# The output product of a Fourier-mixing and gated-FFN kernel: 15 products over three row blocks in place of 7 over two

## The chip, the cores and the metric

The kernel runs on one core of a Trainium2 chip. The metric is the device time of one execution in microseconds (us), the median of three runs: 2009.69 us for the kernel before (2009.16 to 2014.03). All arithmetic is fp32.

## What is computed

The input `x` is (8, 3008, 256): 8 batches of 3008 rows. A two-dimensional Fourier transform over rows and features is taken and its real part kept; the 24064 rows that result go through a gated feed-forward layer with 1536 hidden features.

```
X = np.fft.fft(x, axis=1)
X = np.fft.fft(X, axis=2)
x = X.real.astype(np.float32).reshape(B * S, D)
gate = 1.0 / (1.0 + np.exp(-(x @ w_gate)))
val = x @ w_val
return (gate * val @ w_out).astype(np.float32)
```

## The kernel before

**Symmetry.** Row k and row 3008-k of the transform share their work. For each batch the kernel makes three arrays over k = 0..1504 (1505 columns, features on the partitions): P (`pk`), Q (`qk`) and E (`ek`), where E is the one feature that folding 256 features to 128 leaves over; it is the same in all partitions. The transform over features is merged into the gate and value weights once, at the start (`merge`, L247), giving `G1`, `G2` and the per-feature factors `ge`, which a small DMA takes from row 0 of `G2` (L257). With A = G1'P + ge E and B = G2'Q, the pre-activations of row k are A+B and those of row 3008-k are A-B.

**Chunks and iterations.** The 1505 columns of a batch are cut into chunks of CH = 256 (five of 256, one of 225). For each chunk the main loop (from L691) runs over 12 tiles of 128 hidden features: one iteration `i` per batch, chunk and tile, 576 in all. TensorE and the other engines get their instructions in the order in which this loop writes them, so each engine's queue is in that order. An iteration does:

- `seed` (L447): ScalarE (VectorE in the first chunk) writes ge E into a PSUM bank `pf`, two iterations ahead; gate and value share the bank. `psx` has four such banks.
- `front_a` (L458): TensorE adds G1'P, so that the bank holds A.
- `twice` (L463): ScalarE copies 2A to SBUF (`ae`).
- `front_b` (L469): TensorE adds G2'Q: the bank holds A+B.
- `gate_a` (L474), for the tile before: ScalarE's sigmoid of the gate half, VectorE's 2A-(A+B) = A-B (`z`, L484) and the product gate x value (`h`, L485). `gate_b` (L487): the second sigmoid (L492) and product (`h`, L493), for the mirrored row.

**The output product.** Two feature tiles make a pair. For a pair the output product has 2 row blocks (k and 3008-k) x 2 feature tiles x 2 output halves = 8 matrix products of 128x128 by 128xCH; the kernel takes 7 by the Strassen-Winograd scheme. Four sums per pair of the `h` blocks are made on GpSimd (`sf`, L495 to L499), the weight sums once in `forms` (L260) on GpSimd. `back` (L508) issues the 7 matmuls in two parts, 3 and 4, over the two iterations 2p+4 and 2p+5, into four PSUM banks `po` that accumulate over the chunk's six pairs.

**The end of a chunk.** `finish` (L528): ScalarE copies the products from PSUM to `c` (L522, L580); then a list `later` is worked off one entry per iteration: five sums on GpSimd (L582 to L586), four 32x32-block transposes on VectorE (`flip`, L540) and stores. For the last chunk of all the sums are made on VectorE, from PSUM (L566 to L575).

**Beside it.** The next batch's input is folded on GpSimd, one operation per iteration (`fold_ops`, L282 to L311), and once per batch TensorE makes the next P and Q in one burst (`whole`, L383), in the `po` banks. In the first 50 us, and during the first chunk, the weights are unpacked, merged and turned into their sums. In the start, `half` (L344) also runs matmuls of `dt` against itself into the unused columns of the banks `ev` and `od`.

An fp32 matmul shows in the profile as two instructions, each with its own weight load; below each of them is called a pass. Almost all matmuls bear L102, the line of the helper `mm`.

Of the kernel before, what the change touches and what calls it, by code (L numbers as in the profile page):

```python
# [45 lines left out]

NQ = 6
NP = 126
HP = 64
HUGE = float((2 ** 24 - 1 - 2 ** 20) * 2.0 ** -7)  # L50
# [3 lines left out]
def kernel(  # L54
# [21 lines left out]
    CH = 256  # L76
# [5 lines left out]
    assert F % WC == 0 and D == WC and NFT % 2 == 0 and stab.shape == (NP, 2, NQ, NE + NO)  # L82
# [9 lines left out]
    app = ctx.enter_context(tc.tile_pool(name="app", bufs=3))  # L92
    zp = ctx.enter_context(tc.tile_pool(name="zp", bufs=3))
    hp = ctx.enter_context(tc.tile_pool(name="hp", bufs=3))
    sp = ctx.enter_context(tc.tile_pool(name="sp", bufs=2))
    cp = ctx.enter_context(tc.tile_pool(name="cp", bufs=2))
    op = ctx.enter_context(tc.tile_pool(name="op", bufs=2))
    psx = ctx.enter_context(tc.tile_pool(name="psx", bufs=4, space=PSUM))
# [50 lines left out]
    wf = const.tile([P, NPR, 7, P], F32, name="wf")  # L149
# [7 lines left out]
    ed = dram.tile([B - 1, NK], F32, name="ed")  # L157
# [23 lines left out]
    def weight_load(j):  # L181
# [7 lines left out]
        def some(n, pool, tag):  # L189

            key = tag, (j - 6) // 3 if tag == "c7" else 0
            if key not in shared:
                shared[key] = pool.tile([P, n, 2 * WC], F32, name=f"w{tag}", tag=tag)
            return shared[key]

        if j < KEEP:
            pool, tag = ((zp, "z"), (pqp, ("pk", "qk", "ek")[j % 3]), (op, "os"), (sp, "sf"))[
                j // 3 if j < 6 else j // 2 - 1]
            raw = pool.tile([P, 2, WC, 2], I32, name="raw", tag=tag)
            if j < 6:  # L200
                pool, tag = ((app, "ae"), (hp, "h"))[j // 3]
                ws = pool.tile([P, 2, WC], F32, name="ws", tag=tag)
            else:
                ws = some(3, cp, "c7")[:, (j - 6) % 3].rearrange("p (c f) -> p c f", c=2)
        else:
            both = some(12, xp, "x4")
            r, i = (j - KEEP) % 3 * 2, 6 + (j - KEEP) % 6
            raw = both[:, r : r + 2].rearrange("p a n -> p (a n)").bitcast(I32).rearrange(
                "p (c f w) -> p c f w", c=2, w=2)
            ws = both[:, i].rearrange("p (c f) -> p c f", c=2)  # L210
# [28 lines left out]

    def weight_use(j, other=None):  # L240
        w, c = jobs[j]
        if w == 2:
            forms(WS.pop(j), c)
        else:
            merge(WS.pop(j), w, c, other)
# [14 lines left out]
    def forms(ws, c):  # L260

        w = ws.rearrange("p f (a h j) -> p f h a j", h=2, j=TB)
        f = wf[:, c].rearrange("p m (a j) -> p m a j", j=TB)
        sub = lambda o, a, b: nc.gpsimd.tensor_tensor(o, a, b, op=ALU.subtract)
        nc.scalar.copy(f[:, 0:2], w[:, :, 0])
        nc.scalar.copy(f[:, 2], w[:, 1, 1])
        sub(f[:, 4], w[:, 0, 1], w[:, 0, 0])
        sub(f[:, 6], w[:, 1, 1], w[:, 0, 1])
        sub(f[:, 5], w[:, 1, 1], f[:, 4])
        sub(f[:, 3], w[:, 1, 0], f[:, 5])  # L270
# [73 lines left out]
    def half(w, d, blk, sn, other=None):  # L344
# [3 lines left out]
        full = [bank(name, other and other[i]) for i, name in enumerate(("ev", "od"))]  # L348
        ev, od = [sum_[:, 0:n] for sum_ in full]

        def sums(*qs):
            for q in sorted(qs, key=lambda q: q % 2):
                mm((ev, od)[q % 2], w(q), ST[0][0:NP, int(sn), q, c0 : c0 + n], q < 2, q >= NQ - 2)
            if other is None and NQ - 1 in qs:

                for sum_ in full:
                    mm(sum_[:, n:], dt[:, 0, 0:P], dt.rearrange("p c d -> p (c d)")[:, n:], False, True)
# [25 lines left out]
    def whole(b, blk, what):  # L383
        _, then, both = seq_group(b, blk, what, (2, 1) if what else (3, 0))
        both()
        return then()

    def seq_start(b):
        PQE[b] = (pqp.tile([P, NK], F32, name="pk", tag="pk"),
                  pqp.tile([P, NK], F32, name="qk", tag="qk"),  # L390
                  pqp.tile([P, NK], F32, name="ek", tag="ek"))
        if b:
            nc.sync.dma_start(out=PQE[b][2], in_=ed[b - 1 : b, :].to_broadcast([P, NK]))
# [15 lines left out]
    def e_sums():  # L409


        ps = bank("pe", 3)
# [8 lines left out]
        er = cp.tile([P, NK], F32, name="er", tag="c7")[0:m]  # L421
# [5 lines left out]
        def rest():  # L427
# [3 lines left out]
            nc.scalar.dma_start(out=ed, in_=er)  # L431
# [3 lines left out]
    chunks = [(k0, min(CH, NK - k0)) for k0 in range(0, NK, CH)]  # L435
    pairs = [(b, c, i) for b in range(B) for c in range(len(chunks)) for i in range(NPR)]
    H, SF = {}, {}

    def cut(i):
        b, c, _ = pairs[i // 2]  # L440
        k0, n = chunks[c]
        f = i % (2 * NPR)
        return PQE[b], slice(k0, k0 + n), n, f, slice(f * P, (f + 1) * P)

    PF, AP, Z = {}, {}, {}

    def seed(i):  # L447

        (_, _, ek), ks, n, f, _ = cut(i)
        PF[i] = bank("pf").rearrange("p (g n) -> p g n", g=2)[:, :, 0:n]  # L450
        for g in range(2):
            if i < 2 * NPR:
                nc.vector.tensor_scalar(out=PF[i][:, g], in0=ek[:, ks],  # L453
                                        scalar1=ge[:, g, f : f + 1], scalar2=None, op0=ALU.mult)
            else:
                nc.scalar.activation(PF[i][:, g], ek[:, ks], AF.Copy, scale=ge[:, g, f : f + 1])  # L456

    def front_a(i):  # L458
        (pk, _, _), ks, _, _, fs = cut(i)
        for g in range(2):  # L460
            mm(PF[i][:, g], G1[:, g, fs], pk[:, ks], False, True)

    def twice(i):  # L463

        n = cut(i)[2]
        AP[i] = app.tile([P, 2, CH], F32, name="ae", tag="ae")[:, :, 0:n]
        nc.scalar.activation(AP[i], PF[i], AF.Copy, scale=2.0)  # L467

    def front_b(i):  # L469
        (_, qk, _), ks, _, _, fs = cut(i)  # L470
# [3 lines left out]
    def gate_a(i):  # L474

        n = cut(i)[2]
        p, fh = i // 2, i % 2
        z = Z[i] = zp.tile([P, 3, CH], F32, name="z", tag="z")[:, :, 0:n]
        if fh == 0:
            H[p] = hp.tile([P, 2, 2, CH], F32, name="h", tag="h")[:, :, :, 0:n]  # L480
            SF[p] = sp.tile([P, 4, CH], F32, name="sf", tag="sf")[:, :, 0:n]
        pf = PF.pop(i)
        nc.scalar.activation(z[:, 2], pf[:, 0], AF.Sigmoid)  # L483
        nc.vector.tensor_tensor(z[:, 0:2, ::-1], AP.pop(i), pf, op=ALU.subtract)  # L484
        nc.vector.tensor_tensor(H[p][:, fh, 0], z[:, 2], pf[:, 1], op=ALU.mult)  # L485

    def gate_b(i):  # L487

        p, fh = i // 2, i % 2
        z, h, s = Z.pop(i), H[p], SF[p]  # L490
        tt = nc.gpsimd.tensor_tensor
        nc.scalar.activation(z[:, 0], z[:, 0], AF.Sigmoid)  # L492
        nc.vector.tensor_tensor(h[:, fh, 1], z[:, 0], z[:, 1], op=ALU.mult)  # L493
        if fh == 0:
            tt(s[:, 2], h[:, 0, 0], h[:, 0, 1], op=ALU.subtract)  # L495
        else:
            tt(s[:, 0], h[:, 0, 1], h[:, 1, 1], op=ALU.add)  # L497
            tt(s[:, 1], s[:, 0], h[:, 0, 0], op=ALU.subtract)  # L498
            tt(s[:, 3], h[:, 1, 0], s[:, 1], op=ALU.subtract)  # L499


    SLOT = {1: (3, 0), 2: (0, 0), 6: (0, 1), 5: (1, 0), 7: (1, 1), 4: (2, 1), 3: (2, 0)}
    ORDER = ((1, 2, 4), (6, 3, 7, 5))
    FIRST = {1, 2, 4, 7}
    PO = []
    later = []

    def back(p, part):  # L508
        b, c, i = pairs[p]
        n = chunks[c][1]  # L510
        if part == 0 and i == 0:
# [257 lines left out]
```

## Time and profile before

| what | value |
|---|---|
| time, median of 3 | 2009.69 us |
| profiled span | 2006.7 us |
| first iteration of the main loop starts at | 51.0 us |
| second chunk (iteration 12) starts at | 114.5 us |
| one full chunk afterwards, 180 passes of 256 columns | 38.8 us |
| a batch's last chunk, 180 passes of 225 columns, the first of them still of 256 | 34.9 us |
| a burst for the next P and Q | 11.9 us |
| last matmul ends, last store lands | 1999.3 us, 2006.7 us |

The page lists, for each engine, its busy time and, for each group of instructions, how many there were, the busy time, the mean duration of one, and for how long the engine had stood idle before them. A matmul's duration in it includes the pipeline behind the array; what a stream of matmuls costs is read from the distance between their starts. VectorE is DVE there, ScalarE ACT, GpSimd POOL; PEld are TensorE's weight loads.

### The profile page before, as it was taken

Reading aid. Unit: us, or ns where it says so; the run is one execution under the profiler, and the core shown is the slowest. Engines: PE = TensorE matmul, PEld = TensorE weight load, DVE = VectorE, ACT = ScalarE, POOL = GpSimd, SP = SyncE. Lnnn points to the kernel's source line nnn. Section 1 sums busy time; section 2 is a strip of 40 time slices with the busy share of each in tenths; the row PEclk is TensorE's granted clock in tenths of the full one; section 3 lists DMA queues with packets and bytes.
Section 4 is the critical chain, followed back from the end, with each engine's and each line's share of the span. In section 5 each row is a group of like instructions: output and inputs, shape, how many; then the busy total and the mean of one; then the engine's idle time right before and its main releaser. Section 6 shows DMA issues by size and latency. Waiting matters only on the chain.

```text
span 2006.7 us, 27514 instructions
## 1 busy us (share of the span) xinstructions
PE 1971.3 (98%) x9520; PEld 1740.7 (87%) x9520; DVE 1093.4 (54%) x2093; ACT 1332.4 (66%) x3156; POOL 1285.5 (64%) x1704
## 2 busy tenths in 40 slices
PE   6899999999999999999999999999999999999998
PEld 4688789888998889888898888988899888998888
DVE  7655546554555456554565545555455544554555
ACT  3566657675777567775677656766577665777765
POOL 3577757774786457864677646876477754655554
PEclk9999999999999999999999999999999999999999
DMA  7253412112011020202011021111200000000001
GB/s 266 81 128 82 151 32 102 49 29 74 11 47 47 27 74 17 72 18 90 11 42 52 13 88 22 43 41 37 74 11 11 20 27 12 11 20 12 11 17 26
DMA packets 160811, 100.29 MB, mean 50 GB/s; under 512 B 128419, under 2 KB 151715, under 8 KB 157994
## 3 DMA queue, kind: packets, MB, share of 16 engines
q1 hardware_dynamic: 158850, 98.00, 16.8%
q8 instruction: 75, 1.23, 0.2%
q10 hardware_dynamic: 1822, 0.54, 0.1%
q14 instruction: 64, 0.52, 0.1%
HBM read 73.74 MB, written 50.17 MB: 62 GB/s over the span
## 4 chain that ended last, share of the span: by engine, by line
PE 96%; DMA 2%; DVE 1%; ACT 1%; issue 0%; ACTq 0%; DVEq 0%
PE pf L102 48%; PE po L102 42%; PE ev L102 4%; DMA ge<-G 1%; PE ps L102 1%; DMA st<-in_stab_dram 1%; PE od L102 0%; DVE pf L453 0%; DMA raw<-in_moe_w_gate_dram 0%; DVE z L484 0%; ACT ae L467 0%; PE pe L102 0%; ACT z L492 0%; ACT G L254 0%; ACT z L483 0%
## 5 line engine op out<-in xcount | busy, mean ns | idle before, releaser
L484 DVE TENSOR_TENSOR z<-ae,pf 128x512 f32<-128x512 f32 (+1 forms) x576 | 389.6, 676 | 615.3 <-ACT z L483 615.2
L102 PE MATMUL pf<-pk,G 128*128 128x256 f32 (+1 forms) x2304 | 582.7, 375 | 6.0 <-DVE pf L453 6.0
L102 PE MATMUL pf<-qk,G 128*128 128x256 f32 (+1 forms) x2304 | 582.9, 375 | 5.2 <-ACT ae L467 5.2
L456 ACT ACTIVATE pf<-ek,ge 128x256 f32<-128x256 f32 (+1 forms) x1128 | 532.1, 472 | 18.3
L102 PE MATMUL po<-sf,wf 128*128 128x256 f32 (+1 forms) x2304 | 534.6, 375 | 0.0
L497 POOL TENSOR_TENSOR sf<-h 128x256 f32<-128x256 f32 (+1 forms) x288 | 206.8, 718 | 474.5 <-DVE h L493 474.5
L467 ACT ACTIVATE ae<-pf 128x512 f32<-128x512 f32 (+1 forms) x576 | 339.2, 589 | 248.2 <-PE pf L102 248.1
L102 PEld LDWEIGHTS pf<-pk,G 128*128 128x128 f32 x2304 | 436.7, 190 | 59.3 <-DVE pf L453 7.0
L102 PEld LDWEIGHTS pf<-qk,G 128*128 128x128 f32 x2304 | 438.0, 190 | 57.0 <-ACT ae L467 7.2
L102 PEld LDWEIGHTS po<-sf,wf 128*128 128x128 f32 x2304 | 437.7, 190 | 49.8 <-POOL sf L499 0.4
L493 DVE TENSOR_TENSOR h<-z 128x256 f32<-128x256 f32 (+1 forms) x576 | 348.1, 604 | 190.4 <-ACT z L492 188.6
L102 PE MATMUL po<-h,wf 128*128 128x256 f32 (+1 forms) x1728 | 413.7, 375 | 1.6 <-ACT a L429 1.6
L483 ACT ACTIVATE z<-pf 128x256 f32<-128x256 f32 (+1 forms) x576 | 218.2, 379 | 259.8 <-PE pf L102 253.3
L102 PEld LDWEIGHTS po<-h,wf 128*128 128x128 f32 x1728 | 328.8, 190 | 39.2 <-ACT a L429 2.0
L495 POOL TENSOR_TENSOR sf<-h 128x256 f32<-128x256 f32 (+1 forms) x288 | 206.4, 717 | 139.6 <-PE po L102 58.8
L492 ACT ACTIVATE z<-z 128x256 f32<-128x256 f32 (+1 forms) x576 | 233.1, 405 | 17.4 <-DVE z L484 17.3
L485 DVE TENSOR_TENSOR h<-z,pf 128x256 f32<-128x256 f32 (+1 forms) x576 | 235.1, 408 | 0.0
L498 POOL TENSOR_TENSOR sf<-sf,h 128x256 f32<-128x256 f32 (+1 forms) x288 | 208.2, 723 | 22.6
L499 POOL TENSOR_TENSOR sf<-h,sf 128x256 f32<-128x256 f32 (+1 forms) x288 | 207.5, 721 | 22.6
L102 PE MATMUL ev<-st,x 63*128 63x376 f32 (+4 forms) x372 | 97.7, 414 | 6.0 <-DVE x L292 5.8
L102 PE MATMUL od<-st,x 63*128 63x376 f32 (+4 forms) x372 | 96.8, 412 | 0.0
L102 PEld LDWEIGHTS ev<-st,x 63*128 63x128 f32 (+1 forms) x372 | 66.2, 187 | 32.8 <-DVE x L292 6.2
(98 smaller groups left out, 938.7 us busy)
## 6 DMA issues: line engine op xcount, KB each, us to landing
x<-xr SPq DMA_DIRECT2D x14, 1536.0 KB
out_dram<-os SPq DMA_DIRECT2D x288, 64.0 KB
xr<-in_xf_dram SPq DMA_DIRECT2D x14, 768.0 KB
xr<-in_xf_dram SPq DMA_DIRECT2D x35, 256.0 KB
ek<-ed SPq DMA_DIRECT2D x7, 752.5 KB
out_dram<-os SPq DMA_DIRECT2D x92, 56.0 KB
x<-in_xf_dram SPq DMA_DIRECT2D x2, 1512.0 KB
tr<-in_stab_dram SPq DMA_DIRECT2D x2, 1129.5 KB
```

The lines of the kernel that those rows point to most:

```text
L102: nc.tensor.matmul(o, l, r, start=start, stop=stop, skip_group_check=True)
L456: nc.scalar.activation(PF[i][:, g], ek[:, ks], AF.Copy, scale=ge[:, g, f : f + 1])
L467: nc.scalar.activation(AP[i], PF[i], AF.Copy, scale=2.0)
L483: nc.scalar.activation(z[:, 2], pf[:, 0], AF.Sigmoid)
L484: nc.vector.tensor_tensor(z[:, 0:2, ::-1], AP.pop(i), pf, op=ALU.subtract)
L485: nc.vector.tensor_tensor(H[p][:, fh, 0], z[:, 2], pf[:, 1], op=ALU.mult)
L492: nc.scalar.activation(z[:, 0], z[:, 0], AF.Sigmoid)
L493: nc.vector.tensor_tensor(h[:, fh, 1], z[:, 0], z[:, 1], op=ALU.mult)
L495: tt(s[:, 2], h[:, 0, 0], h[:, 0, 1], op=ALU.subtract)
L497: tt(s[:, 0], h[:, 0, 1], h[:, 1, 1], op=ALU.add)
L498: tt(s[:, 1], s[:, 0], h[:, 0, 0], op=ALU.subtract)
L499: tt(s[:, 3], h[:, 1, 0], s[:, 1], op=ALU.subtract)
```

## The change

Three feature tiles now make a group, and the 2n rows of a chunk are cut into three row blocks of R = 2n/3 rows. A group's output product is 3 row blocks x 3 feature tiles x 2 output halves = 18 matrix products of 128x128 by 128xR, for which a scheme with 15 products is used. It is meant to lower the number of columns that TensorE streams for an output row. So that rows divide by three, chunks have 252 columns (the last of a batch 246).

What goes with it:

- 13 sums of `h` blocks per group on GpSimd (`H_SUMS`), of R elements; 11 sums and 4 copies of weights per group (`W_SUMS`, `W_COPIES`), once.
- `back` in three parts of five products, over iterations 3p+5 to 3p+7. The products fill five PSUM banks, so three are left for `pf`.
- At the end of a chunk 20 sums of R elements (`C_SUMS`) on VectorE in place of five on GpSimd; `later` is worked off three entries per iteration. ScalarE copies five banks instead of four.
- E: from the second chunk on each chunk gets its own rows of E by a DMA (`e_rows`), eight iterations ahead. In the first chunk there is no seed: E stands in row 0 of Q, so that `front_b` adds it, and VectorE makes A in SBUF (`part`).
- The filling matmuls of `dt` are gone, `app` and `zp` have two buffers in place of three, `cp` and `op` one in place of two, and the staging of the weights (`home`) uses other buffers. The folding is spread evenly over 60 iterations (42 for the first two).

```diff
+H_SUMS = {1: ((9, 3, 0, 0), (10, 3, 6, 0), (11, 7, 1, 0), (12, 7, 4, 0), (13, 4, 9, 0), (14, 6, 11, 0),
+              (15, 4, 6, 1)),
+          2: ((11, 8, 11, 0), (12, 8, 12, 0), (9, 5, 9, 0), (10, 10, 5, 0), (16, 2, 11, 0),
+              (16, 9, 16, 0))}
...
+PRODUCTS = ((0, 12), (1, 11), (4, 9), (6, 4), (2, 13), (5, 5), (13, 0), (8, 6), (11, 2), (12, 8), (9, 3),
+            (10, 10), (14, 1), (15, 7), (16, 14))
+PLACE = (0, 1, 2, 5, 3, 4, 6, 7, 8, 9, 10, 11, 14, 13, 12)
+C_SUMS = (((8, 1, 8, 0), (1, 1, 0, 0), (3, 3, 1, 0), (0, 0, 10, 1), (4, 4, 0, 1), (1, 6, 2, 0),
+           (4, 4, 1, 0), (10, 14, 8, 1), (7, 7, 10, 0), (11, 0, 11, 0), (11, 11, 5, 0), (5, 5, 7, 1)),
+          ((9, 9, 8, 0), (9, 13, 9, 1), (9, 9, 2, 0), (12, 9, 12, 0), (12, 11, 12, 1), (14, 9, 14, 0),
+           (11, 11, 6, 0), (13, 13, 11, 1)))
...
-    CH = 256
+    NG = NFT // 3
+    CH = 252
+    NB = 1 + max(b // 3 for b in PLACE)
...
-    psx = ctx.enter_context(tc.tile_pool(name="psx", bufs=4, space=PSUM))
+    psx = ctx.enter_context(tc.tile_pool(name="psx", bufs=8 - NB, space=PSUM))
...
+        for i, (a, b, op) in enumerate(W_SUMS):
+            nc.gpsimd.tensor_tensor(f[:, i], block(a), block(b), op=(ALU.subtract, ALU.add)[op])
+        for i, (a, sign) in enumerate(W_COPIES):
+            nc.scalar.mul(f[:, len(W_SUMS) + i], block(a), float(sign))
...
-            if other is None and NQ - 1 in qs:
-
-                for sum_ in full:
-                    mm(sum_[:, n:], dt[:, 0, 0:P], dt.rearrange("p c d -> p (c d)")[:, n:], False, True)
...
+        EK[i // NFT] = ekp.tile([P, CH], F32, name="ek", tag="ek")[:, 0:n]
+        nc.sync.dma_start(out=EK[i // NFT], in_=ed[b : b + 1, k0 : k0 + n].to_broadcast([P, n]))
...
+        for g in range(2 if i >= NFT else 0):
+            nc.scalar.activation(PF[i][:, g], EK[i // NFT], AF.Copy, scale=ge[:, g, f : f + 1])
...
+        if i >= NFT:
+            nc.scalar.activation(AP[i], PF[i], AF.Copy, scale=2.0)
+            return
         for g in range(2):
+            nc.vector.scalar_tensor_tensor(out=AP[i][:, g], in0=pqe[2][:, ks],
+                                           scalar=ge[:, g, f : f + 1], in1=PF[i][:, g],
+                                           op0=ALU.mult, op1=ALU.add)
...
+        for dst, a, b, op in H_SUMS.get(fh, ()):
+            nc.gpsimd.tensor_tensor(block(p, dst), block(p, a), block(p, b),
+                                    op=(ALU.subtract, ALU.add)[op])
...
+        for at_, (hb, wb) in list(enumerate(PRODUCTS))[part * 5 : part * 5 + 5]:
+            t, j = divmod(PLACE[at_], 3)
+            mm(PO[t][:, j * R : (j + 1) * R], wf[:, g, wb], block(p, hb), g == 0 and at_ % 3 == 0,
+               g == NG - 1)
+            if g == NG - 1 and at_ % 3 == 2:
...
+                nc.scalar.copy(C[0][:, 3 * t * R : 3 * (t + 1) * R], PO[t][:, 0 : 3 * R])
...
+            nc.vector.tensor_tensor(*v, op=(ALU.subtract, ALU.add)[op])
...
+        for h in range(2):
+            later.extend([lambda x=x: sum_(*x) for x in C_SUMS[h]])
+            later.append(lambda h=h: flip(0, h))
+            later.append(lambda h=h: (flip(1, h), h and (store(0), store(1))))
...
+    nc.scalar.dma_start(out=ed[0:1], in_=PQE[0][2][0:1])
+    nc.scalar.copy(PQE[0][1][0:1, 0:CH], PQE[0][2][0:1, 0:CH])
...
+        f0, steps = (s0 - 2 * i0, 5 * i0) if b > 1 else (s0 - 4, 42) if b else (i0 + 8, 42)
...
-        if i >= 4:
-            back(i // 2 - 2, i % 2)
+        if i >= 5:
+            back((i - 5) // 3, (i - 5) % 3)
...
-        if later:
-            later.pop(0)()
+        for f in later[0:3]:
+            f()
+        del later[0:3]
...
-    for p in range(len(pairs) - 2, len(pairs)):
-        for part in range(2):
-            back(p, part)
+    for i in range(count, count + 5):
+        back((i - 5) // 3, (i - 5) % 3)
```

## What the change will do, predicted

> **What bounds the kernel now.** I read the page's busy shares and its chain of waits first:
>
> ```profile
> PE 1971.3 (98%) x9520; PEld 1740.7 (87%) x9520; DVE 1093.4 (54%) x2093; ACT 1332.4 (66%) x3156; POOL 1285.5 (64%) x1704
> ...
> PE 96%; DMA 2%; DVE 1%; ACT 1%; issue 0%; ACTq 0%; DVEq 0%
> ```
>
> TensorE is busy for 98% and is 96% of the chain. A busy share could hide stretching, so next the list of waits, for TensorE alone from 130 to 2000 us:
>
> ```profile
> PE po L102 <- ACT a L429: 1.6, 1, 1.6
> PE pf L102 <- ACT ae L467: 1.0, 1, 1.0
> ```
>
> That is all: 2.6 us in 1870. TensorE streams without gaps, and only fewer or shorter passes shorten this stretch, as long as the others keep up. What a pass costs is read from starts in TensorE's timeline, in three windows (start, length, shape, count):
>
> ```profile
> 1001.38 1.03 PE L102 MATMUL pf<-qk,G 128*128 128x256 f32 x4
> 1002.24 1.03 PE L102 MATMUL pf<-pk,G 128*128 128x256 f32 x4
> ...
> 283.34 0.92 PE L102 MATMUL pf<-qk,G 128*128 128x225 f32 x4
> 284.10 0.92 PE L102 MATMUL pf<-pk,G 128*128 128x225 f32 x4
> ...
> 32.89 0.40 PE L102 MATMUL ev<-dt 128*128 128x135 f32 x2
> 33.12 0.39 PE L102 MATMUL od<-dt 128*128 128x135 f32 x2
> 33.35 0.80 PE L102 MATMUL ev<-st,x 126*128 126x377 f32 x2
> ```
>
> Four passes of 256 columns take 0.86 us, 215 ns each; of 225, 0.76 us, 190 each; of 135, 0.46 us, 115 each. All fit columns/1.2 + 2.4 ns (215.7, 189.9, 114.9). The third matters most: passes of 135 columns with a full weight load each still cost what their columns cost, so loads won't bind at 168.
>
> **What the skill says.** The Trainium skill, "TensorE: Matmul & The Clock Gate", section "LDWEIGHTS (loading the stationary operand)", gives columns/1.2, so 107 ns for 128 columns; the profile's load row says 190 ns for one, but the 115 ns spacing agrees with the page. "SBUF — State Buffer", section "Who interferes with whom": a VectorE instruction with two SBUF inputs and a GpSimd instruction that reads SBUF exclude each other. The timeline of all engines agrees:
>
> ```profile
> 1000.57 1.27 POOL L282 TENSOR_TENSOR x<-x 128x510 f32<-128x510 f32 x1
> ...
> 1000.79 1.33 DVE L493 TENSOR_TENSOR h<-z 128x256 f32<-128x256 f32 x1 [0.36 <-ACT z L492]
> ...
> 1004.24 0.42 DVE L493 TENSOR_TENSOR h<-z 128x256 f32<-128x256 f32 x1 [0.36 <-ACT z L492]
> ```
>
> The same product takes 0.42 us alone, and 1.33 when GpSimd is at work, ending 0.28 us after GpSimd's end (1001.84). The change puts 20 such VectorE sums into each chunk, beside more GpSimd sums; this is its risk. "VectorE: DVE Perf Modes", section on the TRN2 errata, gives (N+151)/0.96 ns for an fp32 tensor_tensor: 424 for 256, as here, and by estimate 332 for 168.
>
> **TensorE, the path that sets the end.** Before, a chunk has 12 x 4 x 2 = 96 front and 6 x 7 x 2 = 84 back passes: 180 x 215.7 = 38.8 us, the last of a batch 180 x 189.9 = 34.2; a batch 228.3 us. After, a chunk of 252 has 96 front passes of 252 columns at 212.4 ns = 20.39 us and 4 x 15 x 2 = 120 back passes of 168 at 142.4 = 17.09, together 37.48; the last one (246, R = 164) 96 x 207.4 + 120 x 139.1 = 36.60. A batch: 5 x 37.48 + 36.60 = 224.0. The saving is 4.3 us a batch, **34.5 us** for eight. The bursts for P and Q (11.9 us each) are unchanged.
>
> **ScalarE** keeps seeds, doubling and sigmoids; spaced by their starts 0.96 + 0.50 + 0.58 = 2.04 us an iteration, plus five bank copies of 0.49 a chunk: 2.25 of the 3.12 us that TensorE takes. Hidden. With three `pf` banks a seed waits for VectorE's `h` of three tiles earlier. From TensorE's start of an iteration: sigmoid to 0.6, z to 1.2, h to 1.65, second sigmoid to 2.05, seeds to 3.0. Behind the seeds in ScalarE's queue stand the next sigmoid and the doubling (together 0.97), which `front_b` wants at 5.4; so VectorE may be late by about 1.75 us before TensorE waits. Shorter `app` and `zp` have 2.9 us or more.
>
> **VectorE.** Own work an iteration: 0.60 + 0.41 + 0.43. The 20 sums: ten depend on the one before (332 + 34 ns, the gap in the trace), ten don't (332 - 83, the overlap of independent ones): 6.15 us a chunk; four transposes of 0.43 as before. That is 25 of 37.5 us, but the work is in eight of twelve iterations: 1.44 + 0.1 (for the sigmoid) + 0.92 = 2.5 of 3.12. Then the port: one product and three sums an iteration, each behind the rest of a GpSimd operation. A first one waits some 0.2 us[...], the following sums 0.2 to 0.26: some 0.8, so 3.3 us. VectorE falls behind by 0.2 to 0.25 in each of six iterations, at most 1.4 us, and makes it up in the four light ones: just inside the slack of 1.75.
>
> **GpSimd.** The prices, by shape:
>
> ```profile
> L497 POOL TENSOR_TENSOR sf<-h 128x256 f32<-128x256 f32 x240 | 175.0, 729 | 417.3 <-DVE h L493 417.3
> L497 POOL TENSOR_TENSOR sf<-h 128x225 f32<-128x225 f32 x48 | 31.8, 662 | 57.3 <-DVE h L493 57.3
> L286 POOL TENSOR_TENSOR x<-x 128x6 f32<-128x6 f32 x14 | 3.0, 213 | 0.0
> ```
>
> 213 ns plus 2.05 per element gives 546 for 168, an estimate. Starts in the timeline show independent operations 0.68 apart at a duration of 0.73, dependent ones 0.81. So 504 or 624 ns. Of a group's 13 sums one needs the sum just before: 12 x 0.504 + 0.624 = 6.67 us, against TensorE's 9.37 for a group. The folds are 29.6 us a batch (their rows, over seven), over 60 iterations 1.48 a group; VectorE's turns at the port[...], 1.0. Sum 9.2 of 9.37 us where folding goes on, 9.8 in the 14 groups of the first two folds, spread over 42 iterations; the surplus, 0.45 x 14 = 6 us, is about what five iterations from the last products to their last use leave over (13.9 - 9.2 = 4.7 us). So the wait is 1 to 2 us for those two. The chunk-end sums that leave GpSimd gave 4.9 us a chunk back, counted here.
>
> **Costed at nothing.** The new E transfer is issued eight iterations, 25 us, before its first use and moves 129 KB a chunk on DMA engines that are 17% busy. The single `c` and `os` buffers: a chunk's last transpose is in its twelfth queue slot and the first copy of the next chunk's products three iterations later (9 us); the next transpose, nine iterations after the stores, 28 us. `h` and `sf` are rewritten at least one iteration after their last matmul. The five product banks are copied in three successive iterations, in the order in which they fill, and the next chunk's products fill them in the same order, two iterations after each copy.
>
> **Edges.** Chunk 0 takes 63.5 us, of which TensorE has 53.9 and GpSimd 38.3 busy. GpSimd gets 44 weight sums for 24 (0.47 each: +9) and +8 of `h` sums: 55, still below; bursts of 11 sums delay what is queued behind, the weights' joins, which are used 2 to 3 iterations later: +3 us (0 to +12). The missing filler is 16 x 115 ns, half of it hidden: -1. VectorE's A in chunk 0 replaces its seeds: 0. The tail: from the last pass to the end 7.4 us before; after, one bank copy 0.75, 13 sums 4.1, four transposes 1.5, stores 4.5: 10.9, +3.5. Stalls inside: +4.
>
> Sum: 2009.7 - 34.5 + 3 - 1 + 3.5 + 4 = **1984.7**, say 1984.
>
> **Rivals.** (1) GpSimd becomes the bound. For: 98% full while folding. Against: the price fit is straight. With half of the sums at the dependent 624 ns a group is 13 x 0.564 + 1.48 + 1.0 = 9.8 us, 0.44 over; 20 groups give 8.8 a batch, less 4.7 of slack 4.1, over seven folds 29 us: 2013. With all at 624 it is 10.6: 25 - 4.7 = 20 a batch, 140 us, 2125. I put it at 2040: slower than before. (2) VectorE's waits at the port exceed the slack by some 0.4 us in each of 40 chunks: 16 us, 2000. For: 1.4 of 1.75 is thin. Against: GpSimd is not always busy. (3) Weight loads bind at 168 columns: 190 ns a load would make back passes 190, 48 ns x 120 x 48 = +274 us, 2259; the filler rows speak against it. (4) Chunk 0 turns out with less waiting, as no seed waits for `ge`: -6, 1977.
>
> **Chances.** Main 0.56; (4) 0.10; (2) 0.18; (1) 0.14; (3) 0.02. Range 1973 to 2012: it takes in (4), (2) and the mild end of (1). Faster 0.83, same 0.06, slower 0.11.
>
> **What would show it.** After: back passes of 168 columns 142 ns apart, chunks of 37.5 us, TensorE's waits still a few us after chunk 0, GpSimd about 80% busy with sums near 0.55 us, VectorE products near 0.6 on average. Chunks of 40 us while folding, with TensorE waiting for `sf`, mean (1); with `pf` waiting for ScalarE and that for VectorE, (2); starts 190 apart, (3).

## The result and the profile after

The kernel after takes **2022.11 us**, the median of four runs (2021.5 to 2022.43), beside 2009.59 us for the kernel before (2009.16 to 2014.03): a ratio of 1.0057, 95% interval 1.0039 to 1.0074. It is slower, where 1984 was predicted, and the time lies above the range.

The profiled spans are 2006.7 and 2020.5 us. The starts of the iterations (TensorE's `front_a`) divide them:

| stretch | before | after | difference |
|---|---|---|---|
| start to the first iteration | 51.0 | 50.6 | -0.4 |
| chunk 0 (iterations 0 to 11) | 63.5 | 69.7 | +6.2 |
| iteration 12 to the start of the last one | 1876.0 | 1876.9 | +0.9 |
| start of the last iteration to the last matmul's end | 8.8 | 10.2 | +1.4 |
| last matmul's end to the end | 7.4 | 13.2 | +5.8 |

Two things have to be explained: the third row, where 34 us should have been gained, and some 13 us at the edges.

**The third row.** I compared each iteration's length with what its columns cost by the prediction's fit (columns/1.2 + 2.4 ns). By columns alone this stretch is 34.0 us shorter after. What the iterations take beyond that, called stalls from here on, is 6.8 us before (5.5 of it in the first batch) and 41.7 after, +34.9. By batch, after chunk 0, the stalls of after are 10.7, 8.1, four times 4.9, 3.1, and 0.13 in the last batch, the only one that has no next batch to fold. So the gain is there and is given back, and only while folding goes on.

The page of after, busy shares and chain of waits:

```profile
PE 1953.0 (97%) x11232; PEld 1792.8 (89%) x11232; DVE 1568.4 (78%) x3065; ACT 1395.4 (69%) x3200; POOL 1624.2 (80%) x2873
...
PE 55%; DVE 30%; ACT 11%; issue 2%; DMA 1%; POOL 0%; DVEq 0%; SPq 0%; ACTq 0%; POOLq 0%
```

TensorE still looks busy (a matmul's recorded time, 380 ns for 252 columns, is longer than the 212 ns from one start to the next and covers gaps), but it has gone from 96% to 55% of the chain, and VectorE from 1% to 30%. That is the change's first trace. TensorE's own list of waits from 130 to 2010 us, beside the 2.6 us of before, and two rows of the list of all waits, first of after, then of before:

```profile
PE pf L125 <- ACT ae L508: 18.4, 40, 0.8
PE po L125 <- ACT a L461: 1.6, 1, 1.6
```
```profile
ACT z L546 <- DVE z L533: 260.2, 304, 2.1
...
PEld pf L125 <- ACT ae L508: 34.6, 61, 1.1
```
```profile
ACT z L492 <- DVE z L484: 17.3, 58, 0.7
...
PEld pf L102 <- ACT ae L467: 7.2, 5, 2.4
```

TensorE waits for ScalarE's doubling (`ae`), ScalarE's second sigmoid waits for VectorE's `z` (260.2 us in place of 17.3), and behind that sigmoid in ScalarE's queue stand the seeds and the next doubling. The weight loads' wait for `ae`, 34.6 us in place of 7.2, is nearer to the loss than the matmuls' 18.4, as their recorded times cover part of each gap.

One iteration shows the mechanism. TensorE, VectorE, GpSimd and ScalarE in the chunk from 853.6 us on:

```profile
879.82 1.59 PE L125 MATMUL po<-h,wf 128*128 128x168 f32 x10
881.24 1.01 PE L125 MATMUL pf<-qk,G 128*128 128x252 f32 x4
882.09 1.01 PE L125 MATMUL pf<-pk,G 128*128 128x252 f32 x4
```
```profile
877.66 0.67 DVE L533 TENSOR_TENSOR z<-ae,pf 128x504 f32<-128x504 f32 x1
878.25 0.41 DVE L534 TENSOR_TENSOR h<-z,pf 128x252 f32<-128x252 f32 x1
878.81 0.60 DVE L547 TENSOR_TENSOR h<-z 128x252 f32<-128x252 f32 x1 [0.15 <-ACT z L546]
879.33 2.33 DVE L592 TENSOR_TENSOR c<-c 128x168 f32<-128x168 f32 x3
881.59 0.67 DVE L533 TENSOR_TENSOR z<-ae,pf 128x504 f32<-128x504 f32 x1
```
```profile
879.09 0.72 POOL L552 TENSOR_TENSOR sf<-h,sf 128x168 f32<-128x168 f32 x1
879.89 0.54 POOL L552 TENSOR_TENSOR sf<-sf 128x168 f32<-128x168 f32 x1
880.39 1.09 POOL L347 TENSOR_TENSOR x<-x 128x384 f32<-128x384 f32 x1
```
```profile
880.02 0.59 ACT L508 ACTIVATE ae<-pf 128x504 f32<-128x504 f32 x1
882.29 0.41 ACT L546 ACTIVATE z<-z 128x252 f32<-128x252 f32 x1 [1.69 <-DVE z L533]
882.68 0.98 ACT L494 ACTIVATE pf<-ek,ge 128x252 f32<-128x252 f32 x2
```

TensorE's ten back passes take 1.42 us to the next start, 142 ns each: its part of the change does what it should. VectorE's three sums take 2.33 us beside a GpSimd sum and a fold of 1.09. From one `z` to the next VectorE needs 3.93 us (877.66 to 881.59), where TensorE's iteration is 3.12. ScalarE's second sigmoid then stands idle for 1.69 us, and the seeds start only at 882.68.

The sums and GpSimd's `h` sums by shape (count | busy us, mean ns | idle before), to be set beside the GpSimd prices of before:

```profile
L592 DVE TENSOR_TENSOR c<-c 128x168 f32<-128x168 f32 x800 | 472.2, 606 | 11.0
...
L552 POOL TENSOR_TENSOR sf<-h,sf 128x168 f32<-128x168 f32 x960 | 540.6, 583 | 41.1 <-DVE h L547 40.9
```

GpSimd's sums, at 583 ns, keep near the estimate of 546. VectorE's take 606 against an estimate of 332 alone. Two windows, a chunk while folding goes on and one of the last batch, show what the other engine does to them (columns: length, then busy time and count of TensorE, its loads, VectorE, ScalarE, GpSimd, then clock, DMA share, GB/s; in the second fence line 592 alone):

```profile
853.60:891.70 38.10, 38.05 (x218) 35.39 (x217) 31.27 (x61) 28.39 (x65) 35.17 (x64) 1.00 0.23 59
1813.40:1850.90 37.50, 37.50 (x217) 35.34 (x216) 28.14 (x61) 28.45 (x65) 28.30 (x54) 1.00 0.10 18
```
```profile
853.60:891.70 38.10, 12.64 (x20) 1.00 0.23 59
1813.40:1850.90 37.50, 10.18 (x20) 1.00 0.10 18
```

The same 20 sums take 12.64 us beside folds (632 ns each) and 10.18 without (509). The chunk without folds takes 37.50 us, just as worked out.

**How late is late?** As a measure I take the lag of `z`: from TensorE's start of the next `front_a` to VectorE's start of `z`. On time it is 0.61 us. Before, it stays within 1.6 from the second batch on. The mean over the second chunks of batches 2 to 5 of after (batches counted from 0), by position of the tile in the chunk:

```
position   0    1    2    3    4    5    6    7    8    9    10   11
lag, us   1.06 0.61 0.63 0.98 1.17 1.49 1.82 2.63 2.31 2.09 2.87 2.29
```

In the last batch its maximum is 1.18. The list `later` is worked off in the iterations at positions 4 to 11, and a tile's `z` is made in the iteration after its own, so the `z` of position 4 is the first behind sums.

### The profile page after: what moved, and what is told of

Its sections match the earlier page's. It is cut to its first block, busy times and chain, and to the rows that moved or that the text cites. A ratio compares the mean times of both kernels' runs of the same rounds, so it can differ in the third digit from the quotient of the medians.

```text
span 2020.5 us, 34215 instructions
## 1 busy us (share of the span) xinstructions
PE 1953.0 (97%) x11232; PEld 1792.8 (89%) x11232; DVE 1568.4 (78%) x3065; ACT 1395.4 (69%) x3200; POOL 1624.2 (80%) x2873
## 3 DMA queue, kind: packets, MB, share of 16 engines
q8 instruction: 88, 1.44, 0.3%
## 4 chain that ended last, share of the span: by engine, by line
PE 55%; DVE 30%; ACT 11%; issue 2%; DMA 1%; POOL 0%; DVEq 0%; SPq 0%; ACTq 0%; POOLq 0%
PE pf L125 28%; PE po L125 21%; DVE c L592 17%; DVE z L533 6%; ACT z L546 5%; DVE h L547 5%; PE ev L125 4%; ACT pf L494 2%; ACT ae L508 1%; ACT c L575 1%; DVE os L599 1%; PE ps L125 1%; ACT z L528 1%; PE od L125 1%; DMA x<-in_xf_dram 1%
## 5 line engine op out<-in xcount | busy, mean ns | idle before, releaser
L552 POOL TENSOR_TENSOR sf<-h 128x168 f32<-128x168 f32 (+1 forms) x960 | 537.0, 576 | 274.5 <-DVE h L547 272.3
L552 POOL TENSOR_TENSOR sf<-h,sf 128x168 f32<-128x168 f32 (+1 forms) x1152 | 646.1, 580 | 47.6 <-DVE h L547 47.1
L125 PE MATMUL pf<-qk,G 128*128 128x252 f32 (+1 forms) x2304 | 591.8, 380 | 32.6 <-ACT ae L508 18.4
L125 PE MATMUL pf<-pk,G 128*128 128x252 f32 (+1 forms) x2304 | 582.7, 376 | 0.0
L592 DVE TENSOR_TENSOR c<-c 128x168 f32<-128x168 f32 (+1 forms) x960 | 566.2, 605 | 16.9 <-ACT c L575 3.6
L494 ACT ACTIVATE pf<-ek,ge 128x252 f32<-128x252 f32 (+1 forms) x1128 | 536.0, 475 | 18.5 <-DMA ek<-ed 0.2
L533 DVE TENSOR_TENSOR z<-ae,pf 128x504 f32<-128x504 f32 (+1 forms) x564 | 376.4, 667 | 211.1 <-ACT z L528 210.4
L125 PE MATMUL po<-sf,wf 128*128 128x168 f32 (+1 forms) x3072 | 529.9, 305 | 0.0
L125 PE MATMUL po<-h,wf 128*128 128x168 f32 (+1 forms) x2688 | 475.9, 306 | 3.9 <-POOL wf L304 2.2
L125 PEld LDWEIGHTS pf<-qk,G 128*128 128x128 f32 x2304 | 408.0, 190 | 77.0 <-ACT ae L508 34.6
L546 ACT ACTIVATE z<-z 128x252 f32<-128x252 f32 (+1 forms) x576 | 236.4, 410 | 275.4 <-DVE z L533 260.2
L508 ACT ACTIVATE ae<-pf 128x504 f32<-128x504 f32 (+1 forms) x564 | 331.2, 587 | 128.3 <-PE pf L125 121.2
```

Source lines behind the costliest of these rows:

```text
L125: nc.tensor.matmul(o, l, r, start=start, stop=stop, skip_group_check=True)
L494: nc.scalar.activation(PF[i][:, g], EK[i // NFT], AF.Copy, scale=ge[:, g, f : f + 1])
L533: nc.vector.tensor_tensor(z[:, 0:2, ::-1], ap, pf, op=ALU.subtract)
L552: nc.gpsimd.tensor_tensor(block(p, dst), block(p, a), block(p, b), op=(ALU.subtract, ALU.add)[op])
L592: nc.vector.tensor_tensor(*v, op=(ALU.subtract, ALU.add)[op])
```

## The experiments

In all runs the kernel before ran beside on the same chip (2010 to 2011 us). "Stalls" are those from iteration 12 to the last, counted as above: 6.8 before, 41.7 after.

**Theories.** A: VectorE's chunk-end sums, slowed by GpSimd at the shared port, make `z` late, and with three `pf` banks TensorE must then wait. B: three `pf` banks cost by themselves, whatever the sums do. C: VectorE has too many instructions, each with a turn at the port. D: the sums would be better off on GpSimd, as before.

### Sums without turns at the port; no folds; three banks alone; fewer instructions

The first kernel has 20 transposes of 160 columns with one SBUF input in place of the 20 sums of each chunk; the sums are left out.

```diff
-            nc.vector.tensor_tensor(*v, op=(ALU.subtract, ALU.add)[op])
+            src = v[1] if a != dst else v[2]
+            nc.vector.transpose(v[0][:, 0 : 5 * TB], src[:, 0 : 5 * TB])
```

> The changed kernel, with each of the 20 chunk-end sums on VectorE replaced by a 32x32-block transpose of 160 columns: about the same time on VectorE (0.33 us), but one SBUF input instead of two, so no turn at the port shared with GpSimd. The sums themselves are left out, so the output is not the reference's. Port theory (VectorE's sums wait for GpSimd at the shared port, VectorE falls behind, and TensorE waits for what ScalarE does after it): the stalls after chunk 0, 42 us by the distances between iterations, nearly vanish: 1980 us, 1975 to 1988; chunk 0 and the tail stay. Own-work theory (the sums are simply too much work for VectorE): 2015 to 2022. Bank theory (three pf banks are too few): 2015 to 2022. GpSimd theory (GpSimd is too full to deliver its sums in time): about 2005, as only VectorE's turns are taken off it.

Measured: 1986.13 us (1984.71 to 1989.99), ratio 0.9868 (0.9833 to 0.9903); stalls 6.7. Iteration 12 to the last takes 1841.8 us in place of 1876.9. TensorE's waits from 130 us on are back to those of before:

```profile
PE po L125 <- ACT a L461: 1.6, 1, 1.6
PE pf L125 <- ACT ae L508: 0.6, 1, 0.6
```

The second leaves out the folds of batches 1 to 7 (their input is then not the right one), and keeps the sums:

```diff
         def folds(f0, steps, b=b):
             ops = fold_ops(b + 1, 2)
-            for i, f in enumerate(ops):
-                at(f0 + i * steps // len(ops), f)
+            del ops
```

> The changed kernel without the folding of batches 1 to 7 on GpSimd (left out; the output is then not the reference's). GpSimd loses 30 us of 248 per batch. Port theory and GpSimd theory: all chunks run like those of batch 7, which have 0.1 us of stall in six chunks: 1980 us, 1975 to 1986. Own-work theory and bank theory: 2015 to 2022.

Measured: 1986.57 us (1985.19 to 1989.52), ratio 0.987 (0.9828 to 0.9911); stalls 8.4. Either partner of the collision taken away gives nearly the whole 35 us back: at this pace the loss needs both, which is theory A. In the second kernel all 20 sums are still there, at 522 ns on average in place of 606; the transposes of the first take 337, about the 332 estimated for a sum alone. So what stalls TensorE is the time that the sums take beyond their own, on top of VectorE's other work.

The third is the kernel before with three rotating `pf` banks; the fourth bank serves the start only.

```diff
-    psx = ctx.enter_context(tc.tile_pool(name="psx", bufs=4, space=PSUM))
+    psx = ctx.enter_context(tc.tile_pool(name="psx", bufs=3, space=PSUM))
+    psy = ctx.enter_context(tc.tile_pool(name="psy", bufs=1, space=PSUM))
```

> The kernel before with three pf banks in place of four (the fourth bank is used in the start alone). Bank theory: the stalls of the changed kernel come with it, 2009.6 + 30 to 40 = 2040 to 2050. Port, own-work and GpSimd theory: little, 2009 to 2016, where the surplus is in chunk 0, whose merges use the same banks.

Measured: 2014.67 us (2010.93 to 2018.77, 20 runs) beside 2010.14, ratio 1.0014 (1.0003 to 1.0026). Iteration 12 to the last is 1876.0 us, the same as before; the surplus of the profiled run lies ahead of it, 4.8 in the start and 1.9 in chunk 0. Theory B falls: three banks cost nothing where VectorE is on time. That they set how late it may be is the prediction's reckoning; no run has the late sums with four banks.

The fourth makes the 20 sums in 11 instructions, nine of them of two sums each over strided views, two entries of `later` in an iteration.

```diff
+C_PAIRS = ((((8, 1), (1, 1), (8, 0), 0), ((0, 10), (0, 14), (10, 8), 1), ((3, 7), (3, 7), (1, 10), 0),
+            ((1, 11), (6, 0), (2, 11), 0), ((4, 11), (4, 11), (1, 5), 0), ((4, 5), (4, 5), (0, 7), 1)),
...
-        for f in later[0:3]:
+        for f in later[0:2]:
             f()
-        del later[0:3]
+        del later[0:2]
```

> The changed kernel with the 20 chunk-end sums in 11 instructions: nine of them make two sums at once (2 x 168 elements, strided views of c), and two entries of the list are worked off per iteration. VectorE's turns at the port fall from 20 to 11 a chunk, its own time for the sums from about 6.2 to 5.4 us. Port theory: the stalls fall from 42 to about 10 us: 1990, 1983 to 1998. Own-work theory: with 0.8 us less of 25 a chunk, but spread wider, 2005 to 2015. Bank theory: 2018 to 2022. GpSimd theory: 2012 to 2020.

Measured: 1990.19 us (1988.33 to 1991.63), ratio 0.9885 (0.985 to 0.9919); stalls 8.2. The same sums, with nothing left out, no longer stall TensorE. But two things were changed here, the number of instructions (C) and the pace at which `later` is worked off.

### Turns or pace?

Two kernels tell them apart. One has the single sums, spread over ten iterations with at most three and mostly two entries:

```diff
-        for f in later[0:3]:
+        m = (0, 0, 0, 0, 3, 2, 2, 3, 2, 2, 3, 2)[i % i0] if i % i0 > 1 else (3, 2)[i % i0]
+        for f in later[0:m]:
             f()
-        del later[0:3]
+        del later[0:m]
```

> The changed kernel with the same 20 chunk-end sums, one by one, but spread over ten iterations (4 to 13 of the chunk's clock, two or three entries each) in place of eight. If it is the lag built up in a row that costs, it falls by a fifth to a third: stalls of 42 become 20 to 30 us, 2003 to 2012. If each turn at the port cost TensorE directly, nothing changes: 2021.

Measured: 1989.36 us (1988.99 to 1993.43), ratio 0.9899 (0.9884 to 0.9914); stalls 8.6. The other has the pairs at three entries in an iteration, as after:

```diff
-        for f in later[0:2]:
+        for f in later[0:3]:
             f()
-        del later[0:2]
+        del later[0:3]
```

> Sums in pairs (11 instructions), but with three entries of the list per iteration as in the changed kernel, so that the pace is the only difference to the run with two per iteration (1990). Port theory by number of turns: three turns of 0.75 us an iteration in four to five iterations is as dense as the single sums were (3 x 0.6), so stalls come back in part: 1995 to 2008. If the number of turns a chunk alone counts, as with two: 1988 to 1992.

Measured: 2016.0 us (2013.08 to 2024.53, 12 runs), ratio 1.003 (1.0018 to 1.0041); stalls 36.8. Both miss what was expected of them, to opposite sides, and together they settle it: with GpSimd's work unchanged the pace decides, and not the number of turns. Theory C falls. Groups of line 592 in the spread kernel, and of the paired sums at two and at three entries:

```profile
L592 DVE TENSOR_TENSOR c<-c 128x168 f32<-128x168 f32 x800 | 465.2, 589 | 13.7
```
```profile
L606 DVE TENSOR_TENSOR c<-c 128x336 f32<-128x336 f32 x360 | 279.2, 775 | 10.0 <-ACT pf L498 0.5
```
```profile
L606 DVE TENSOR_TENSOR c<-c 128x336 f32<-128x336 f32 x360 | 261.0, 725 | 10.0 <-ACT pf L498 0.5
```

The single sums in the spread kernel are hardly cheaper than in the kernel after (589 against 606 ns), and a pair costs 20 to 28% more than one sum; yet the first doesn't stall and pairs at three an iteration do. VectorE's other work in an iteration is 1.44 + 0.1 us by the prediction, and 0.13 more for the second product, which takes 560 ns on average where 0.43 stands in that sum. With the mean duration of the sums, against the 3.12 us of an iteration, and the largest lag in batches 2 to 5 (an estimate in the first three columns: durations overlap a little, and some entries are transposes):

| kernel | sums in an iteration, us | with the rest, us | less 3.12 | largest lag, us | stalls, us |
|---|---|---|---|---|---|
| after | 3 x 0.61 = 1.8 | 3.5 | +0.4 | 4.1 | 41.7 |
| pairs, three entries | 3 x 0.725 = 2.2 | 3.8 | +0.7 | 3.2 | 36.8 |
| pairs, two entries | 2 x 0.775 = 1.5 | 3.2 | +0.1 | 1.9 | 8.2 |
| spread | 2.4 x 0.59 = 1.4 | 3.1 | 0 | 2.2 | 8.6 |
| transposes in place of sums | 3 x 0.34 = 1.0 | 2.7 | -0.4 | 1.55 | 6.7 |

The kernels that stall have lags of 3 us and more; those with at most 2.2 don't. Between them lies the limit that the prediction had put at 1.75 us beyond the on-time 0.61, about 2.4.

### The sums on another engine

```diff
-            nc.vector.tensor_tensor(*v, op=(ALU.subtract, ALU.add)[op])
+            (nc.vector if last else nc.gpsimd).tensor_tensor(*v, op=(ALU.subtract, ALU.add)[op])
```

> The changed kernel with the 20 chunk-end sums on GpSimd, where the five sums of the kernel before were (all chunks but the last). GpSimd then has 28.2 + 20 x 0.51 = 38.5 us of sums a chunk, and 4.9 to 5.9 of folding in five of six, against TensorE's 37.5. GpSimd becomes the bound: about 6 us more in each of some 35 chunks, part of it caught up in the bursts for P and Q: 2130 us, 2070 to 2220. If the port and not GpSimd's own time were all that counts, it would be near 1985.

Measured: 2476.44 us (one run), far above what I expected; stalls 487.6. GpSimd's load is a large part of it: GpSimd is busy for 90% from 1000 to 1100 us and makes up 58% of the chain of waits. But it also stands idle, and the list of waits shows in which order the engines wait:

```profile
DVE os L599 <- POOL c L592: 574.5, 120, 11.9
ACT z L546 <- DVE z L533: 542.0, 227, 11.4
...
PE pf L125 <- ACT ae L508: 351.5, 78, 9.7
```

VectorE's chunk-end transposes wait in its queue for GpSimd's sums, up to 11.9 us, and the next `z` stands behind them; the lag of `z` reaches 12 us. VectorE is busy for 43% here, and its wait is dear because the next link of the main chain is queued behind it. How the loss divides between that and GpSimd's load was not measured. Theory D falls: of the two places, VectorE is the better one.

The kernel before with its own five sums moved to VectorE:

```diff
-        tt = (nc.vector if last else nc.gpsimd).tensor_tensor
+        tt = nc.vector.tensor_tensor
```

> The kernel before with its five chunk-end sums on VectorE (two of 512, three of 256 elements) in place of GpSimd, one per iteration: one part of the change alone. Port theory: VectorE waits for GpSimd once more in five of twelve iterations, but with 3.2 us an iteration and one such sum VectorE stays in time: no change, 2006 to 2013. If moving the sums to VectorE were bad in itself, it would be slower, 2020 or more.

Measured: 2009.92 beside 2010.96 us, ratio 0.999 (0.9983 to 0.9997): next to nothing. In the chunks of 256 columns its sums show no waiting on average: a product of 256 elements alone takes 0.42 us, and these take 0.41 to 0.42.

```profile
L582 DVE TENSOR_TENSOR c<-c 128x512 f32<-128x512 f32 x40 | 28.6, 714 | 1.3
...
L583 DVE TENSOR_TENSOR c<-c 128x256 f32<-128x256 f32 x40 | 16.8, 419 | 0.0
```

So moving sums to VectorE doesn't cost by itself; five a chunk, one an iteration, fit. But these sums hardly meet folds: the kernel before runs them in positions 3 to 7 of a chunk, and its `quiet` issues the folds in the others. Where a fold still reaches into position 3, beside the first sum of a batch's last chunk, that sum of 450 elements takes 1.6 us; another of the same size takes 0.6. The change gave this separation up when it spread the folds evenly. Whether folds kept away from the chunk-end sums would have saved the 35 us no run has tested.

### Chunk 0 and a better kernel

In chunk 0 TensorE of after waits mostly for VectorE's A (`ae`, line 511 in place of ScalarE's 508). First the rows of before, from 48 to 115 us, with the seeds (line 453), then those of after, from 50 to 121:

```profile
PE pf L102 <- DVE pf L453: 6.0, 5, 3.1
PE pf L102 <- ACT ae L467: 4.2, 4, 2.0
```

```profile
PE pf L125 <- DVE ae L511: 12.2, 9, 3.4
PE po L125 <- POOL wf L304: 2.2, 1, 2.2
```

In the loop, `part` stands behind `gate_a` of the tile before, so VectorE makes `z` and `h` first. Moved ahead in the first 12 iterations:

```diff
         front_a(i)
+        if i < NFT:
+            part(i)
         if i:
             gate_a(i - 1)
-        part(i)
+        if i >= NFT:
+            part(i)
```

> The changed kernel with VectorE's making of A in the first chunk (part) put ahead of the gate work of the tile before in the queues of the first 12 iterations. If chunk 0 is longer than before (69.7 against 63.5 us) because front_b waits for VectorE's A behind z and h of the tile before, chunk 0 falls by 4 to 8 us: 2015 to 2018 us. If GpSimd's sums of the weights or the merges set it, it stays within 1 us: 2021 to 2023.

Measured: 2018.86 us (2016.46 to 2029.8, 10 runs), ratio 1.0049 (1.0032 to 1.0067). Chunk 0 takes 65.0 us in place of 69.7; the waits are

```profile
PE pf L125 <- DVE ae L511: 6.2, 5, 2.7
PE po L125 <- POOL wf L304: 5.2, 2, 5.1
```

The wait for A halves, and 3 us of it come back as a wait for the weight sums, GpSimd's burst. So a good part of chunk 0's +6.2 us is the order of VectorE's queue, and the weight sums were nearly hidden behind that. The size is rough: in the other kernels whose chunk 0 is that of after it took 67.7 to 70.6 us.

Pairs at two entries, A first, and in the tail the store of rows k ahead of the last transpose, with the partial rows' stores on the other queue of two:

```diff
         for h in range(2):
-            later.append(lambda h=h: (flip(1, h), h and (store(0), store(1))))
+            if last and h:
+                later.append(lambda: store(0))
+            later.append(lambda h=h: (flip(1, h), h and (last or store(0), store(1))))
```

> Sums in pairs (11 instructions, two entries per iteration), VectorE's A first in chunk 0, and for the last chunk of all the stores of the rows k issued ahead of the last transpose and the partial rows shared between two DMA queues. From 1990: -5 for chunk 0 if that reading is right, -3 for the tail, whose 12 stores on one queue take 4.7 us to issue: 1982, 1978 to 1988.

Measured: **1983.55 us** (1982.26 to 1986.08), ratio 0.986 (0.9838 to 0.9881). It beats both kernels, the one before by 1.4%. Chunk 0 65.3, stalls 8.0, the tail 12.4. The tail's edit brought 0.9 us where 3 was expected. TensorE's waits from 118 to 1950 us:

```profile
PE po L129 <- ACT a L465: 1.6, 1, 1.6
PE pf L129 <- ACT ae L512: 0.6, 1, 0.6
```

Two attempts to take more from it. GpSimd's 13 sums of a group in nine instructions, four of them of two sums:

```diff
+H_PAIRS = {1: (((9, 10), (3, 3), (0, 6), 0), ((11, 12), (7, 7), (1, 4), 0), ((13,), (4,), (9,), 0),
+               ((14,), (6,), (11,), 0), ((15,), (4,), (6,), 1)),
+           2: (((11, 12), (8, 8), (11, 12), 0), ((10,), (10,), (5,), 0), ((9, 16), (5, 2), (9, 11), 0),
+               ((16,), (9,), (16,), 0))}
```

> The best version so far (1983.6) with GpSimd's 13 sums of h blocks in nine instructions, four of them making two sums at once. TensorE has no stalls left in the steady part, so GpSimd's 0.8 us less per group should bring nothing there; in chunk 0 GpSimd delays the weight sums (5.1 us of TensorE waiting for wf), and 3 us less of its work ahead of them should bring 1 to 3 us: 1981, 1979 to 1985.

Measured: 1983.59 us (1982.54 to 1992.73), ratio 0.9881 (0.9853 to 0.9909). Chunk 0 falls to 62.8, but stalls rise to 11.1. This kernel brackets the limit closely: in batches 2 to 5 each first chunk has a largest lag of 2.40 us and loses nothing, each fifth one has 2.62 and loses 0.24. The same, with the weight sums one iteration earlier as well:

```diff
-        at(2 * c + (-3, -2, 1)[w], lambda j=j: weight_use(j))
+        at(2 * c + (-3, -2, 0)[w], lambda j=j: weight_use(j))
```

> The same with the weight sums of each group issued one iteration earlier (two for 2c+1 in place: at 2c), so that the third group's are ahead of the h sums of iteration 8 in GpSimd's queue. The wait of TensorE for wf, 5.1 us in iteration 11, should go: 1978, 1974 to 1982. If chunk 0 is bound by VectorE's joins instead, no change from the run above.

Measured: 1985.95 us (1982.09 to 1988.52), ratio 0.9876 (0.9859 to 0.9893). Chunk 0 is 58.7 us and the wait for the weight sums falls from 5.3 to 0.3, but 4.8 us come back two chunks later (stalls 14.6). The trace shows where: at 179.5 us ScalarE's seeds for the fourth chunk wait 4.6 us for their rows of E (`ek`), the new transfer that the prediction costed at nothing; in the kernel after it cost 0.2 us once. The last three kernels aren't told apart by their times.

## Why the prediction was wrong

**What held.** *The saving in columns*, -34.5 in all: -34.0 in the stretch from iteration 12 to the last. *The price of a pass*: 142 ns at 168 columns, unstalled chunks 37.50 us; rival (3), weight loads, fell. *GpSimd*: 80% busy, sums near 0.58 where 0.546 was estimated, spaced 0.50 or 0.62 (medians) where 0.504 or 0.624 was put down; TensorE doesn't wait for `sf`, and rival (1) fell. *The slack*: "VectorE may be late by about 1.75 us before TensorE waits"; kernels with lags up to 2.2 us don't stall, those with 3 and more do, and in the kernel with GpSimd's sums in nine instructions the limit lies between 2.40 and 2.62; 0.61 + 1.75 is 2.36. *The port*: the Trainium skill, "SBUF — State Buffer", section "Who interferes with whom", says that a VectorE instruction with two SBUF inputs contends with GpSimd's reads and that one with at most one SBUF input, outside the 2-port modes, doesn't. The run with transposes agrees (below).

**What failed: the term "Stalls inside: +4".** It measured +34.9: 30.9 of the 37.5 us by which the result (+12.5) differs from the sum (-25). The edges hold the rest (the profiled spans differ by 13.8 and not 12.5, so the stretches add up to 1.3 more). VectorE's lateness had been put at nothing, as "just inside the slack of 1.75". Rival (2) named the mechanism, and the last section of the prediction its signature, "with `pf` waiting for ScalarE and that for VectorE", which is what the profile shows. At 16 us the rival was under-sized too. Rival (4) fell: chunk 0 became longer, not shorter. In the VectorE paragraph two steps carried the error.

1. "VectorE falls behind by 0.2 to 0.25 in each of six iterations, at most 1.4 us". So the largest lag would be 0.61 + 1.4 = 2.0 us; it measured up to 4.1. The wait of a single sum was about right: 606 less 332 is 0.27 us, where 0.2 to 0.26 had been put down. But the sum averages the waits over iterations. With the measured means it is +0.4; and the iterations aren't alike. In the second chunks of batches 2 to 5 VectorE is busy for 3.1, 3.3, 3.3, 3.7, 2.7, 2.9 and 3.8 us from the `z` of positions 3 to 9 to the next; in that chunk of the last batch, without folds, for at most 3.2. In the chunk shown above GpSimd has eight folds, of 0.72 to 1.09 us, in five places, some singly and some two in a row; the iteration in which the three sums meet the one of 1.09 falls behind by 0.81 (3.93 against 3.12, the timeline above). The lag rises unevenly, by 0.8 from position 6 to 7 and from 9 to 10, and reaches 2.9 on average in the second chunks, 4.1 in the sixth. A limit is passed by the peak, not by the mean.

2. "plus five bank copies of 0.49 a chunk ... Hidden." They are hidden as a load, but they stand in ScalarE's queue ahead of the seeds and the next sigmoid, at positions 2 to 4, just before and as VectorE's sums begin:

```profile
865.18 1.05 ACT L575 COPY c<-po 128x504 f32<-128x504 f32 x2
866.11 1.01 ACT L494 ACTIVATE pf<-ek,ge 128x252 f32<-128x252 f32 x2
867.05 0.36 ACT L528 ACTIVATE z<-pf 128x252 f32<-128x252 f32 x1
```

The sigmoid that `z` waits for starts behind two copies and two seeds. So `z` is already 0.98 and 1.17 late, in place of 0.61, at positions 3 and 4, in the last batch too (0.98 and 1.15), and just so in the kernels that have transposes or nothing in place of VectorE's sums there. 0.35 to 0.55 of the 1.75 us of slack is gone before the sums add to it. The kernel before shows 1.19 at position 3 of its chunks, behind its four copies, so this could have been read ahead of the change. No run moved the copies.

Together, as an estimate: 1.1 at the start and 0.4 an iteration pass 2.4 after four, and the mean lag does so at position 7 (2.63); pairs at three entries, with 0.7 an iteration, pass it after two; with two entries or the spread the lag hardly grows, and its largest values are 1.9 and 2.2. How the 34.9 us divide between the two steps was not measured.

**The edges**, +5.5 predicted (3 - 1 + 3.5), +13.0 measured. *Chunk 0*, "+3", measured +6.2: the step "VectorE's A in chunk 0 replaces its seeds: 0" is the one that failed. In chunk 0 the kernel before makes a seed one iteration ahead of its use (later two); A is wanted within its own iteration, and behind `z` and `h` in VectorE's queue it came late; chunk 0 was 4.7 us shorter when A was put first. *The tail*, "13 sums 4.1 ... stores 4.5", +3.5, measured +5.8, with one more deferred part of the last group (+1.4). VectorE's timeline at the end:

```profile
2006.29 3.83 DVE L592 TENSOR_TENSOR c<-c 128x164 f32<-128x164 f32 x12 [3.57 <-ACT c L575]
2010.17 0.77 DVE L599 STREAM_TRANSPOSE os<-c 128x256 f32<-128x256 f32 x2
2010.87 2.58 DVE L592 TENSOR_TENSOR c<-c 128x164 f32<-128x164 f32 x8
2013.48 0.77 DVE L599 STREAM_TRANSPOSE os<-c 128x256 f32<-128x256 f32 x2
```

All 20 sums, 6.4 us, lie behind the copies rather than 13, only the first 1.0 us of them ahead of the last matmul's end at 2007.3; and from the last transpose to the end it is 6.3 us, not 4.5.

## What to carry to other kernels

Where queues run in order and a ring of buffers gives some slack, the thing to work out is the largest lag over a stretch, with what the other engines put into their own queues at the same moment, and not the mean load of each engine: a kernel whose engines are 78% and 80% busy lost 35 us here. Work that is deferred should be spread so that no iteration exceeds the bound engine's time, at the durations that the instructions have when their partner at the port is busy; the same sums spread over ten iterations, or in pairs at two entries, cost under 2 us. And when an operation replaces another on the same engine at equal cost, ask whether it is wanted sooner, and what stands ahead of it.

## What was unexpected of the hardware

Transposes with one SBUF input take no part in the collision. In the kernel with transposes in place of sums, and in the kernel after (min/median/max ns):

```profile
L593 DVE STREAM_TRANSPOSE c<-c x960: 295/337/347, 133.0 to 1975.5; 128x160 f32<-128x160 f32 x192
```
```profile
L592 DVE TENSOR_TENSOR c<-c x960: 282/582/1399, 135.6 to 2013.1; 128x168 f32<-128x168 f32 x160, 128x164 f32<-128x164 f32 x32
```

960 transposes never exceed 347 ns beside GpSimd's folds and sums, while two-input sums of about the same size range from 282 to 1399. The second surprise is that two sums in one instruction cost 725 to 775 ns, 120 to 170 more than a single one's 606, and that this saving alone didn't help: at the unchanged three entries an iteration it raised VectorE's load per iteration and kept the stalls.
